# The last output chunk of a Sinkhorn-attention + bilinear-FFN kernel, written as one 128x512 piece instead of a 384-column and a 128-column piece

## The chip, the core and the metric

The kernel runs on one core of a Trainium2 chip. The metric is the device time in microseconds (us) of one execution; for the kernel before it is the median of three runs. A profiled execution gives the trace that all rows below come from.

## What is computed

The kernel computes block-sorted attention and feeds its output to a bilinear feed-forward layer. Batch 4, 8 heads, 768 positions, head size 64; the feed-forward layer sees 3072 tokens of width 512 and a hidden width of 1536.

```
P = sort_net                          # (4, 8, 8, 8), one 8x8 matrix a head
for _ in range(5):                    # Sinkhorn
    P = exp(P - max(P, -1)); P /= sum(P, -1) + 1e-9; P /= sum(P, -2) + 1e-9
k_sorted, v_sorted = P mixed over the 8 blocks of 96 positions of k and of v
attn = softmax(q_block @ k_sorted_block.T / 8)       # each block of 96 on its own
x    = (attn @ v_sorted_block), heads side by side    # (3072, 512)
out  = ((x @ w_a) * (x @ w_b)) @ w_out                # (3072, 512) float32
```

## The kernel before

All matmul operands are bfloat16; sums are float32 in PSUM. The batches 0 to 3 go one after the other through attention and feed-forward, and the attention of the next batch is woven between the feed-forward steps of the present one by a fixed order written out in the kernel (`paced`). The order of every engine is that of the code: the whole program stands in a manual schedule. GpSimd issues the loads, SyncE (SP) the transposes by DMA and the stores.

Batch 3 has no attention left to weave in, so its feed-forward runs alone. It has 24 `ffn_ab` steps (12 chunks of the hidden width times 2 halves of 384 tokens: eight 128x384 matmuls into two PSUM tiles `pf` at L343, a copy by ScalarE at L363, a product by VectorE into `hT` at L364) and then six `ffn_out` steps, one for each chunk `c` = 0 to 5 of 128 tokens. These six are the end of the kernel, and only they bear on what follows.

For chunks 0 to 4 of batch 3, `ffn_out` makes 12 accumulating matmuls (KO = 12) of 512 columns into one PSUM tile `po` (L386), copies the 128x512 float32 result to the SBUF tile `o_sb` (through the helper `copy`: L161 when ScalarE does it, for even `c`; L163 when VectorE does it, for odd `c`), and SyncE issues one DMA of 256 KB to the output (L399). `po` comes from the pool `psF` with four buffers, `o_sb` has three.

For the last chunk (batch 3, `c` = 5), `ffn_out` calls `ffn_last` instead (L380, L381). It handles the 512 output columns as two pieces, one after the other: columns 0 to 383 with 12 matmuls of 384 columns (L373), a ScalarE copy and a DMA on SyncE's queue (L377); then columns 384 to 511 with 12 matmuls of 128 columns, a VectorE copy and a DMA on ScalarE's queue (L377). It is the only DMA of the program that ScalarE issues.

After the last instruction of the program's own, the closing code follows (the profile gives it line L630): SyncE waits for the DMA semaphores one after the other, and then the engines meet, clear semaphores and meet again.

Of the kernel before, what the change touches and what calls it, by code (L numbers as in the profile page):

```python
# [9 lines left out]
FP32 = mybir.dt.float32  # L10
# [6 lines left out]
def _ap(t: bass.AP, extra_offset, pattern):  # L17
    return bass.AP(tensor=t.tensor, offset=t.offset + extra_offset,
                   ap=[list(p) for p in pattern])
# [3 lines left out]
def kernel(  # L23
# [11 lines left out]
    nc = tc.nc  # L35
    P = 128
    B, H, S, D = q.shape
# [3 lines left out]
    DMODEL = H * D  # L41
# [4 lines left out]
    NCH = S // P  # L46
    HP = H // 2
    KA = DMODEL // P
    KO = DFF // P
# [16 lines left out]
    ffp = ctx.enter_context(tc.tile_pool(name="ffp", bufs=2))  # L66
    psA = ctx.enter_context(tc.tile_pool(name="psA", bufs=2, space=PSUM))
    psF = ctx.enter_context(tc.tile_pool(name="psF", bufs=4, space=PSUM))
# [31 lines left out]
    w_out_sb = const.tile([P, KO, DMODEL], BF16, name="w_out_sb")  # L100
# [58 lines left out]
    def copy(eng, out, in_):  # L159
        if eng == "act":  # L160
            nc.scalar.copy(out=out, in_=in_)  # L161
        else:
            nc.vector.tensor_copy(out=out, in_=in_)  # L163
# [170 lines left out]
    hTs = {}  # L334
# [29 lines left out]
        nc.vector.tensor_mul(out=hT[:, m, t * HW:(t + 1) * HW], in0=a_sb,  # L364
                             in1=ab[1][:, 0:HW])

    def ffn_last(b, c):
        hT = hTs[b]
        rows = out[b * S:(b + 1) * S, :].rearrange("(p c) n -> c p n", c=NCH)
        for n0, n1, eng, queue in ((0, 384, "act", nc.sync), (384, DMODEL, "dve", nc.scalar)):  # L370
            po = psF.tile([P, 512], FP32, tag="F", name="po")
            for m in range(KO):
                nc.tensor.matmul(po[:, 0:n1 - n0], lhsT=hT[:, m, c * P:(c + 1) * P],  # L373
                                 rhs=w_out_sb[:, m, n0:n1], start=(m == 0), stop=(m == KO - 1))
            o_sb = ffp.tile([P, 512], FP32, tag="o_sb", name="o_sb", bufs=3)
            copy(eng, o_sb[:, 0:n1 - n0], po[:, 0:n1 - n0])
            queue.dma_start(out=rows[c][:, n0:n1], in_=o_sb[:, 0:n1 - n0])  # L377

    def ffn_out(b, c):
        if b == B - 1 and c == NCH - 1:  # L380
            ffn_last(b, c)  # L381
            return
        hT = hTs[b]
        po = psF.tile([P, DMODEL], FP32, tag="F", name="po")
        for m in range(KO):
            nc.tensor.matmul(po, lhsT=hT[:, m, c * P:(c + 1) * P], rhs=w_out_sb[:, m, :],  # L386
                             start=(m == 0), stop=(m == KO - 1))
        o_sb = ffp.tile([P, DMODEL], FP32, tag="o_sb", name="o_sb", bufs=3)
        copy("act" if c % 2 == 0 else "dve", o_sb, po)
        if b == 0:  # L390
            h, u = divmod(c, 3)
            for c2 in range(2):
                nc.sync.dma_start(
                    out=_ap(out, (h * PH * NCH + 2 * u + c2) * DMODEL,
                            [[NCH * DMODEL, PH], [1, DMODEL]]),
                    in_=o_sb[c2 * PH:(c2 + 1) * PH])
        else:
            rows = out[b * S:(b + 1) * S, :].rearrange("(p c) n -> c p n", c=NCH)
            nc.sync.dma_start(out=rows[c], in_=o_sb)  # L399


    with tc.manual_schedule(engines={ET.PE, ET.Pool, ET.SP}):
        with tc.manual_schedule(engines={ET.Activation, ET.DVE}):
# [7 lines left out]
            for it in range(5):  # L411
# [7 lines left out]
                if it == 2:  # L419
                    with nc.allow_low_precision("sum of one one and zeros"):  # L420
                        nc.vector.reduce_sum(
                            out=mask, in_=_ap(ident, 0, [[P, P], [1, CG], [CG, NB]]),
# [3 lines left out]
                if it > 0:  # L426
                    nc.tensor.matmul(heat[0:NB, 1, 0:NB], lhsT=rsum, rhs=rsum,
                                     start=True, stop=True)
# [8 lines left out]
                else:  # L437
                    nc.vector.tensor_mul(
                        out=p_fin.bitcast(BF16).rearrange("h (i j u) -> h i j u", i=NB, j=NB),
# [160 lines left out]
        for b in range(B):  # L600
            ab = [lambda m=m, t=t, b=b: ffn_ab(b, m, t)
                  for m in range(KO) for t in range(2) if b > 0 or t == 1]
            po = [lambda c=c, b=b: ffn_out(b, c) for c in range(NCH)]
            paced(ab, po, units_full(b + 1) if b + 1 < B else [], 3 if b == 0 else 2)
# [30 lines left out]
```

## Time and profile before

| what | value |
| --- | --- |
| median of 3 runs | 250.99 us (250.99 to 251.01) |
| the profiled execution's own time | 250.99 us |
| its span, first to last instruction | 249.2 us |
| what lies around the span | 1.8 us |
| granted TensorE clock | 1.000 of full |
| PE busy / VectorE busy / ScalarE busy | 239.0 us (96%) / 112.8 us (45%) / 102.8 us (41%) |
| stores by SyncE, 256 KB each (L399) | 17, landing 2.0 us after the issue (median) |

The profiled execution took as long as the median of the runs, so a sum made against its trace can be read as a change of the median. In rows of the profile, the engine comes first, then the line, the operation and the tiles (`out<-in`); a trailing q (SPq, ACTq) means the engine's sequencer, which issues DMAs and waits for semaphores. "Landing" is the time from the start of a DMA's issue to the update of its semaphore.

### The profile page before, as it was taken

The page shows a single profiled execution, that of the slowest core. Times are in us where ns is not written, and L with a number is a line of the kernel's source. Part 1 is how long each engine was busy: PE and PEld are TensorE (multiplying, and loading weights), DVE is VectorE, ACT ScalarE, POOL GpSimd, SP SyncE. Part 2 cuts the span into 40 slices and gives each one's busy share as a digit, 9 for nine tenths or more (in the row PEclk, how much of TensorE's full clock was granted, in tenths as well). Part 3 has the DMA queues.
Part 4 walks back from the last instruction along what each step waited for, and adds up shares of the span by engine and source line. Part 5 has one row for each costly group of instructions (what it writes and reads, how often), then busy time and mean ns, then how long its engine had stood idle before and what let it go on. Part 6 is the DMA issues. An engine that isn't in the chain of part 4 may idle for free.

```text
span 249.2 us, 5660 instructions
## 1 busy us (share of the span) xinstructions
PE 239.0 (96%) x2330; PEld 139.8 (56%) x2342; DVE 112.8 (45%) x267; ACT 102.8 (41%) x203; POOL 59.4 (24%) x83
## 2 busy tenths in 40 slices
PE   7789899999999999999999999999999999999994
PEld 2366566666655455666655456666645456655443
DVE  6774546655654323464633334363616144444110
ACT  3365656366633035636343146645440033333001
POOL 8975579439300002305061000000000000000000
PEclk9999999999999999999999999999999999999999
DMA  6999999999832869646584831232134310000122
GB/s 81 198 199 197 197 202 198 207 202 202 98 63 54 168 141 158 95 78 90 85 130 128 201 102 31 45 63 45 33 82 116 121 42 3 0 0 4 42 114 97
DMA packets 49162, 26.85 MB, mean 108 GB/s; under 512 B 25968, under 2 KB 46192, under 8 KB 49136
## 3 DMA queue, kind: packets, MB, share of 16 engines
q0 software_dynamic: 20944, 14.16, 39.0%
q1 hardware_dynamic: 28048, 12.27, 21.3%
q8 instruction: 18, 0.29, 0.5%
q10 hardware_dynamic: 144, 0.07, 0.1%
q14 instruction: 8, 0.07, 0.1%
HBM read 28.32 MB, written 6.29 MB: 139 GB/s over the span
## 4 chain that ended last, share of the span: by engine, by line
PE 90%; DMA 2%; POOL 2%; DVE 2%; issue 1%; ACT 1%; POOLq 0%; DVEq 0%
PE pf L343 50%; PE po L386 24%; PE mix L292 4%; PE o_ps L242 3%; DMA v<-in_v_dram 2%; PE sc L313 2%; PE mixh L192 1%; PE po L373 1%; PE vs_ps L282 1%; PE sc L207 1%; PE vs_ps L219 1%; PE q_ps L271 1%; PE xt_ps L233 1%; DVE hT L364 1%; DVE xph L248 1%
## 5 line engine op out<-in xcount | busy, mean ns | idle before, releaser
L364 DVE TENSOR_TENSOR hT<-a_sb,pf 128x384 bf16<-128x384 bf16 x95 | 52.5, 553 | 73.1 <-PE pf L343 49.2
L343 PE MATMUL pf<-xT,w_a_sb 128*128 128x384 bf16 x380 | 77.9, 327 | 0.0
L343 PE MATMUL pf<-xT,w_b_sb 128*128 128x384 bf16 x380 | 77.4, 326 | 0.0
L363 ACT CAST a_sb<-pf 128x384 bf16<-128x384 f32 x95 | 45.5, 479 | 63.9 <-PE pf L343 42.6
L386 PE MATMUL po<-w_out_sb,hT 128*128 128x512 bf16 x265 | 60.5, 379 | 0.6
L343 PEld LDWEIGHTS <-w_b_sb 128*128 128x128 bf16 x384 | 37.5, 98 | 24.9 <-issue 0.3
L343 PEld LDWEIGHTS <-w_a_sb 128*128 128x128 bf16 x384 | 34.9, 98 | 22.1
L386 PEld LDWEIGHTS <-hT 128*128 128x128 bf16 x276 | 26.4, 98 | 30.2
L161 ACT COPY o_sb<-po 128x512 f32<-128x512 f32 (+1 forms) x13 | 7.5, 577 | 50.5 <-PE po L386 49.1
L163 DVE COPY o_sb<-po 128x512 f32<-128x512 f32 (+1 forms) x12 | 7.9, 658 | 42.5 <-PE po L386 37.0
L318 ACT ACTIVATE eT<-sc 96x768 bf16<-96x768 f32 x24 | 18.1, 803 | 3.2 <-PE sc L313 3.2
L248 DVE TENSOR_TENSOR xp<-o_ps,rec 96x512 bf16<-96x512 f32 x24 | 15.7, 683 | 0.2
L161 ACT CAST kT<-mix 128x384 bf16<-128x384 f32 x24 | 10.3, 482 | 7.9 <-PE mix L292 7.9
L94 POOL DMA_DIRECT2D k<-in_k_dram x16 | 11.6, 728 | 6.1 <-PE pf L343 3.6
L94 POOL DMA_DIRECT2D v<-in_v_dram x16 | 11.6, 726 | 4.8 <-PE pf L343 3.1
L242 PEld LDWEIGHTS <-eT 96*128 96x128 bf16 x256 | 10.3, 97 | 3.3 <-ACT eT L211 0.7
L550 POOL COPY gate<-kT 1x1 bf16<-1x1 bf16 x4 | 0.7, 178 | 47.3 <-ACT kT L161 47.3
L242 PE MATMUL o_ps<-vs,eT 96*128 96x65 bf16 x256 | 11.2, 193 | 0.6 <-ACT eT L211 0.6
L94 POOL DMA_DIRECT2D q<-in_q_dram x12 | 8.7, 724 | 3.2 <-DMA w_out_sb<-in_moe_w_out_dram 1.6
L257 POOL COPY qc<-q 128x768 bf16<-128x768 bf16 x8 | 6.6, 842 | 8.1 <-DMA q<-in_q_dram 8.1
L167 PE MATMUL heat<-warm 128*128 128x512 bf16 x20 | 6.9, 484 | 1.4 <-DVE warm L77 1.3
L211 ACT ACTIVATE eT<-sc 96x768 bf16<-96x768 f32 x8 | 6.5, 808 | 3.3 <-PE sc L207 3.3
(81 smaller groups left out, 162.3 us busy)
## 6 DMA issues: line engine op xcount, KB each, us to landing
out_dram<-o_sb SPq DMA_DIRECT2D x17, 256.0 KB, 2.0
k<-in_k_dram POOLq DMA_DIRECT2D x16, 192.0 KB, 6.5
v<-in_v_dram POOLq DMA_DIRECT2D x16, 192.0 KB, 6.4
q<-in_q_dram POOLq DMA_DIRECT2D x12, 192.0 KB, 7.0
w_a_sb<-in_moe_w_a_dram POOLq DMA_DIRECT2D x6, 256.0 KB, 10.6
w_b_sb<-in_moe_w_b_dram POOLq DMA_DIRECT2D x6, 256.0 KB, 10.7
w_out_sb<-in_moe_w_out_dram POOLq DMA_DIRECT2D x3, 512.0 KB, 10.0
out_dram<-o_sb SPq DMA_DIRECT2D x12, 128.0 KB, 2.4
```

Source lines behind the costliest of these rows:

```text
L94: nc.gpsimd.dma_start(out=to, in_=_ap(t, base, [[W, P], [S * D, 2], [1, W]]))
L161: nc.scalar.copy(out=out, in_=in_)
L163: nc.vector.tensor_copy(out=out, in_=in_)
L167: nc.tensor.matmul(ps[:, 0:cols], lhsT=warm[:, 0:P], rhs=warm[:, 0:cols], start=True, stop=True)
L242: nc.tensor.matmul(o_ps[:, e, i * (D + 1):(i + 1) * (D + 1)], lhsT=eT[:, hf, e, i * BLK:i * BLK + P], rhs=vs[0:BLK, i0 + i, V0 - 1 + e * ( ...
L248: nc.vector.tensor_tensor(out=_ap(xp, i0 * 2 * D, [[nxp * 2 * D, BLK], [D, 2], [2 * D, NBH], [1, D]]), in0=_ap(o_ps, 1, [[1024, BLK], [511 ...
L292: nc.tensor.matmul(mix[e * D:(e + 1) * D, c // 3, c % 3 * P:(c % 3 + 1) * P], lhsT=src2[:, e, c * D:(c + 1) * D], rhs=s_all[:, 2 * g + e], ...
L318: nc.scalar.activation(out=eT[:, hf, :, 0:HB], in_=sc[0:BLK, :, 0:HB], func=AF.Exp, scale=float(scale))
L343: nc.tensor.matmul(pf[:, 0:HW], lhsT=w_sb[:, kc, m * P:(m + 1) * P], rhs=x_cols(b, kc, t), start=(kc == 0), stop=(kc == KA - 1))
L363: nc.scalar.copy(out=a_sb, in_=pf[:, 0:HW])
L364: nc.vector.tensor_mul(out=hT[:, m, t * HW:(t + 1) * HW], in0=a_sb, in1=ab[1][:, 0:HW])
L386: nc.tensor.matmul(po, lhsT=hT[:, m, c * P:(c + 1) * P], rhs=w_out_sb[:, m, :], start=(m == 0), stop=(m == KO - 1))
```

## The change

The function `ffn_last` and its call are taken out. The last chunk then goes through `ffn_out` as chunk 3 of the same batch does: 12 matmuls of 512 columns into one `po`, one VectorE copy of 128x512 (`c` = 5 is odd), and one DMA of 256 KB on SyncE's queue. Nothing else of the program is changed; before this chunk every engine has the same instructions in the same order. ScalarE loses one copy and its one DMA; SyncE issues as many DMAs as before.

```diff
-    def ffn_last(b, c):
-        hT = hTs[b]
-        rows = out[b * S:(b + 1) * S, :].rearrange("(p c) n -> c p n", c=NCH)
-        for n0, n1, eng, queue in ((0, 384, "act", nc.sync), (384, DMODEL, "dve", nc.scalar)):
-            po = psF.tile([P, 512], FP32, tag="F", name="po")
-            for m in range(KO):
-                nc.tensor.matmul(po[:, 0:n1 - n0], lhsT=hT[:, m, c * P:(c + 1) * P],
-                                 rhs=w_out_sb[:, m, n0:n1], start=(m == 0), stop=(m == KO - 1))
-            o_sb = ffp.tile([P, 512], FP32, tag="o_sb", name="o_sb", bufs=3)
-            copy(eng, o_sb[:, 0:n1 - n0], po[:, 0:n1 - n0])
-            queue.dma_start(out=rows[c][:, n0:n1], in_=o_sb[:, 0:n1 - n0])
-
     def ffn_out(b, c):
-        if b == B - 1 and c == NCH - 1:
-            ffn_last(b, c)
-            return
         hT = hTs[b]
         po = psF.tile([P, DMODEL], FP32, tag="F", name="po")
         for m in range(KO):
```

## The prediction

> **What bounds the kernel now.** I read the page's summary first, then the page's chain of work that ended last, then the same chain cut to the last 21 us, then the timeline of the last 8 us, and at last the waits of SyncE and the DMA issues of the closing stretch. The page says that the kernel as a whole is bound by TensorE:
>
> ```profile
> PE 239.0 (96%) x2330; PEld 139.8 (56%) x2342; DVE 112.8 (45%) x267; ACT 102.8 (41%) x203; POOL 59.4 (24%) x83
> PE 90%; DMA 2%; POOL 2%; DVE 2%; issue 1%; ACT 1%; POOLq 0%; DVEq 0%
> L163 DVE COPY o_sb<-po 128x512 f32<-128x512 f32 (+1 forms) x12 | 7.9, 658 | 42.5 <-PE po L386 37.0
> ```
>
> That share says nothing of the edit, which touches only the last chunk. The last row's mean of 658 ns mixes eleven copies of 128x512 with one of 128x128, so I do not use it. The chain, cut to its last 21 us, ends in pieces (start, duration, what) that are TensorE's last matmuls and then VectorE's copy alone:
>
> ```profile
> 243.43 2.63 PE po L373 x24
> 246.06 0.02 issue
> 246.08 0.29 DVE o_sb L163
> ```
>
> The timeline shows what lies beside them:
>
> ```profile
> 240.93 0.69 DVE L163 COPY o_sb<-po 128x512 f32<-128x512 f32 x1 [4.54 <-PE po L386]
> ...
> 243.26 2.78 PE L373 MATMUL po<-w_out_sb,hT 128*128 128x384 bf16 x24
> 243.46 0.59 ACT L161 COPY o_sb<-po 128x512 f32<-128x512 f32 x1 [4.59 <-PE po L386]
> 245.46 0.48 ACT L161 COPY o_sb<-po 128x384 f32<-128x384 f32 x1 [1.41 <-PE po L373]
> 245.96 0.33 SPq L377 DMA_DIRECT2D out_dram<-o_sb  x1
> 246.08 0.29 DVE L163 COPY o_sb<-po 128x128 f32<-128x128 f32 x1 [4.46 <-PE po L373]
> 246.41 0.38 ACTq L377 DMA_DIRECT2D out_dram<-o_sb  x1
> ```
>
> Its rows are start, duration, engine, what, and in brackets the idle time before and who ended it. TensorE runs without a gap into its last matmul; both copies wait for TensorE and not for a buffer. The first piece's copy and store begin 0.6 us before the second piece's copy: they lie beside TensorE's last 12 matmuls. Behind TensorE stand, in order, a copy of 128x128 (0.29 us), an issue, a landing, and the closing code. The waits of SyncE and the issues of the last 24 us say which landing the closing code waits for and how long a store takes:
>
> ```profile
> SPq L630 <- DMA out_dram<-o_sb: 1.5, 2, 1.3
> ```
>
> ```profile
> out_dram<-o_sb SPq DMA_DIRECT2D x5, 256.0 KB, 2.0
> out_dram<-o_sb SPq DMA_DIRECT2D x1, 192.0 KB, 1.9
> out_dram<-o_sb ACTq DMA_DIRECT2D x1, 64.0 KB, 1.6
> ```
>
> SyncE waits twice for output stores at the end (1.5 us in total). By the trace's records the 192 KB store lands at 247.83 us and the 64 KB store at 248.05 us, so the last landing is the small store's, and the span ends at 249.21 us: 1.15 us of closing code behind it. The landings in nanoseconds from issue are 2003 to 2042 for the five 256 KB stores and 1647 for the 64 KB one. So the end is one serial path: TensorE, second copy, its store, closing code. Each term of it is on the path in full.
>
> **The change part by part.** I follow that path and take differences.
>
> *Matmuls.* Before, 24 matmuls: the 384-column ones start 0.1625 us apart and the 128-column ones 0.056 us apart, together 12 x 0.2185 = 2.62 us of starts. After, 12 of 512 columns, which start 0.216 us apart in chunks 0 to 4: 2.59 us. The copy starts behind the last matmul's start by 0.256 us with 128 columns, and by 0.415 us (three copies) or 0.471 us (one, on VectorE) with 512. From the chunk's first matmul at 243.26 us to the copy that is now 246.08 - 243.26 = 2.82 us and then becomes 11 x 0.216 + 0.415 = 2.79 us, or 2.85 us. I take 0.00, with ends -0.03 and +0.03. Half the weight loads fall away (24 become 12); they cost nothing now, because the 24 lie beside matmuls that already run without a gap.
>
> *The last copy.* VectorE's copy grows from 128x128 to 128x512. The trace has both forms: 0.291 us and 0.692 us. Nothing covers it, since TensorE has ended: +0.40 us. The removed ScalarE copy (0.48 us) ended at 245.94 us, before TensorE's end, so taking it out gains nothing.
>
> *Waits for buffers.* The new copy takes the `o_sb` buffer that chunk 2 used, whose store was issued at 238.89 us and landed 2.0 us later, some 5 us before it is wanted. It also follows chunk 4's ScalarE copy, over at 244.05 us. Cost 0, hidden by 2 us or more of TensorE's work.
>
> *The last issue.* SyncE issues in place of ScalarE. Issues on SyncE started 0.024 to 0.028 us behind the end of their copies, ScalarE's 0.032 us: about 0.00. In front of it on SyncE's queue stands only chunk 4's store, issued at 244.07 us, and nothing but the closing code is queued behind it. ScalarE's issue of 0.38 us goes, and nobody waited for it other than through the landing.
>
> *The landing.* One store of 256 KB instead of 64 KB behind the copy. The nearest rows are the five stores of the same size, shape and queue from the same stretch: 2.01 us (median) against 1.65 us. +0.36 us, with ends +0.32 (if the 192 KB store's traffic beside it had held up the small one a little less than I think) and +0.41. The removed 192 KB store ended first and gains nothing. A price well above that would need other traffic; the slowest 256 KB store of the program took 4.6 us, among loads and transposes, and none of those is left at the end.
>
> The page "DMA: Bandwidth & Descriptors" of the Trainium skill, section "Rules for kernel authors", speaks for the change: it says to coalesce many small transfers into one large one. Its section "Anatomy of one DMA" gives about 2.0 us fixed for each DMA of GpSimd's path; if the two stores paid that in series, the change would save 2.0 us there and the sum would be near 249.4 us. The rows speak against that reading: the two landings, 1.87 and 1.65 us long, overlap and together last 2.09 us (245.96 to 248.05), so no fixed cost is paid twice on the path. By that section's other term, bytes over 436 GB/s, the landing would differ by 0.45 us instead of 0.36 and the sum would be 251.87 us (an estimate from that page).
>
> *Closing code.* SyncE checks its eight store semaphores one after the other, about 0.06 us each, in a fixed order. Now the last landing is that of the fourth check, with four to go; after the change SyncE's last store carries the semaphore of the third, with five to go. +0.06 us; ends 0 and +0.06. The rest (1.14 us from the fourth check to the end) stays.
>
> *Sum.* 0.00 + 0.40 + 0.00 + 0.36 + 0.06 = +0.82 us; with the matmul term at its more frequent row (-0.03) it is +0.79 us, which I take. The profiled execution took 250.99 us, the same as the median, so 250.99 + 0.79 = 251.78 us. Adding the low ends gives 250.99 - 0.03 + 0.40 + 0.32 + 0 = 251.68; the high ends give 250.99 + 0.03 + 0.40 + 0.41 + 0.06 = 251.89. About 0.2% (0.5 us) is what a measurement of this kernel can tell from no change, so the sum lies above that bound, not far.
>
> **The rivals.**
>
> *No change that can be told: the larger store costs nothing.* If a landing on quiet queues were all fixed latency, and 1.65 us for the small store only reflected a head start of its queue, just the copy would count: 250.99 + 0.40 = 251.39 us, within 0.2%. For it: 192 KB landed in 1.87 us and 64 KB in 1.65, so most of a landing does not depend on size. Against it: five rows of 256 KB, all at 2.0 us, are longer than both. 8 in 100.
>
> *Faster: ScalarE's DMA queue has a price outside the span.* The change removes the only DMA that ScalarE issues, and with it the queue (144 packets, q10 on the page). If the program pays for a second hardware queue in the 1.8 us around the span, all of that is the most it can save: 250.99 + 0.79 - 1.8 = 250.0 us. It decides from 0.79 + 0.5 = 1.3 us of saving on, that is, if over 70% of the time around the span were that queue's. For it: no row shows what fills that time. Against it: nothing in the span waits for that queue, and its one issue took 0.38 us, 0.05 more than SyncE's. 4 in 100.
>
> *Slower by more: the last store lands late.* If the last 256 KB store took what the slowest did, 4.6 us, the time would be 250.99 + 0.79 + 2.6 = 254.4 us; half of that excess gives 253.1. Against it: the last 21 us hold no other traffic of size. 4 in 100.
>
> *The change does not reach the end.* If another engine finished last, nothing would change. The chain and SyncE's wait for the store exclude it; 1 in 100, counted with the first rival.
>
> **How the numbers follow.** The forecast has 83 in 100: 251.78 us. The range begins at 251.4, where the first rival lies, and goes to 252.0, a tenth above the high ends, for small shifts around the span that no row bounds; it leaves out 1 to 2 in 10. Slower by over 0.2% (above 251.49): the forecast and the late store, 0.87. Within 0.2%: 0.09. Faster: 0.04.
>
> **What would show it right or wrong.** Right: the last VectorE copy has the form 128x512 with 0.69 us and starts within 0.05 us of 246.08; SyncE issues 256 KB about 0.03 us behind its end, near 246.8; it lands 2.0 us later; five checks follow, and the span is 250.0 us. Wrong: a landing under 1.8 us, or a time around the span that is no longer 1.8 us, or a start of the last copy that moved by over 0.1 us, which would mean that something before the last chunk shifted.

## The result, and the profile after

| | before | after |
| --- | --- | --- |
| median of 6 runs each, on one chip | 251.00 us (250.99 to 251.25) | 251.84 us (251.58 to 252.10) |
| profiled execution: time / span | 250.99 / 249.21 us | 251.84 / 250.05 us |
| time around the span | 1.78 us | 1.79 us |

The ratio is 1.0032, with a 95% interval of 1.0019 to 1.0045: the kernel became 0.84 us slower, about 0.3%. The interval leaves out "no change"; its low end, 0.19%, lies just under the 0.2% that one measurement can tell. Run times of one kernel fall into steps some 0.25 us apart, and two of the traces below run 0.27 to 0.28 us later than the kernel before from the 19th microsecond of the span on, long before anything that was changed. So single terms are read from the last chunk's rows and not from run times.

The last pieces of the chain that ended last (start, duration, what), of the kernel after:

```profile
241.53 4.49 PE po L371 x20
246.02 0.04 DVEq L163
246.06 0.04 issue
246.10 0.69 DVE o_sb L163
```

It has the same shape as before: TensorE, then VectorE's copy alone. The last piece is 0.69 us instead of 0.29 us long, and it begins at 246.10 instead of 246.08 us. A new piece of 0.04 us stands ahead of it, VectorE's own sequencer (DVEq). Beside it, rows of the timeline:

```profile
243.46 0.59 ACT L161 COPY o_sb<-po 128x512 f32<-128x512 f32 x1 [4.59 <-PE po L371]
246.10 0.69 DVE L163 COPY o_sb<-po 128x512 f32<-128x512 f32 x1 [4.49 <-PE po L371]
246.82 0.33 SPq L384 DMA_DIRECT2D out_dram<-o_sb  x1
```

No store is issued between 244.4 and 246.82 us, where before 192 KB were on their way from 245.96 us on. The waits of SyncE at the end, and the DMA issues after 245.5 us (queue, count, KB, us to landing):

```profile
SPq L615 <- DMA out_dram<-o_sb: 1.5, 1, 1.5
```

```profile
out_dram<-o_sb SPq DMA_DIRECT2D x1, 256.0 KB, 2.0
```

SyncE now waits once, for the one store, 1.5 us long. It landed 2.017 us behind its issue; the closing code behind it took 1.215 us where it had taken 1.154.

All terms of the path, in us, as the two traces' records have them, from chunk 4's ScalarE copy (243.46 us in both) to the end of the span:

| | before | after | difference | predicted |
| --- | --- | --- | --- | --- |
| from chunk 4's copy to the start of the last copy | 2.620 | 2.645 | +0.025 | -0.03 (+0.03 by the other row) |
| last copy | 0.291 | 0.692 | +0.401 | +0.40 |
| its end to the issue of the last store | 0.032 | 0.027 | -0.005 | 0.00 |
| landing of the last store | 1.647 | 2.017 | +0.370 | +0.36 |
| closing code | 1.154 | 1.215 | +0.061 | +0.06 |
| sum | 5.744 | 6.596 | +0.852 | +0.79 |

The span itself grew by 0.846 us, since chunk 4's copy began 0.006 us earlier. Each trace is one execution, but the rows come back in the traces of the experiments below: a last store of 256 KB lands 2.016 to 2.023 us behind its issue in all five versions that have one, a last one of 64 KB, issued 0.44 to 0.45 us behind another, 1.632 to 1.650 us in three. The closing code takes 1.210 to 1.220 us where five checks follow the last landing, and 1.154 and 1.169 us where four do.

### The profile page after: what moved, and what is told of

Read it like the earlier page. It is cut to its first block, busy times and chain, and to the rows that moved or that the text cites. A ratio compares the mean times of both kernels' runs of the same rounds, so it can differ in the third digit from the quotient of the medians.

```text
span 250.1 us, 5634 instructions
## 1 busy us (share of the span) xinstructions
PE 239.0 (96%) x2318; PEld 139.1 (56%) x2330; DVE 113.2 (45%) x267; ACT 102.3 (41%) x202; POOL 59.4 (24%) x83
## 3 DMA queue, kind: packets, MB, share of 16 engines
HBM read 28.32 MB, written 6.29 MB: 138 GB/s over the span
## 4 chain that ended last, share of the span: by engine, by line
PE 90%; DMA 3%; DVE 2%; POOL 2%; issue 1%; ACT 1%; POOLq 0%; DVEq 0%
PE pf L343 50%; PE po L371 25%; PE mix L292 4%; PE o_ps L242 3%; DMA v<-in_v_dram 3%; PE sc L313 2%; PE mixh L192 1%; PE vs_ps L282 1%; PE sc L207 1%; PE vs_ps L219 1%; PE q_ps L271 1%; PE xt_ps L233 1%; DVE hT L364 1%; DVE xph L248 1%; POOL k L94 1%
## 5 line engine op out<-in xcount | busy, mean ns | idle before, releaser
L371 PE MATMUL po<-w_out_sb,hT 128*128 128x512 bf16 x277 | 63.1, 379 | 0.6
L371 PEld LDWEIGHTS <-hT 128*128 128x128 bf16 x288 | 27.5, 98 | 31.6
L163 DVE COPY o_sb<-po 128x512 f32<-128x512 f32 x12 | 8.3, 691 | 42.6 <-PE po L371 41.4
L161 ACT COPY o_sb<-po 128x512 f32<-128x512 f32 x12 | 7.0, 586 | 49.1 <-PE po L371 49.1
```

## The experiments

The theory: the end is one serial path, and copy, landing and closing checks each count in full. The rivals: a landing does not depend on size; ScalarE's DMA queue has a price around the span; the closing checks or the copy lie beside something else. "Path" below is the stretch of the table's sum, from chunk 4's ScalarE copy to the end of the span: 5.74 us before, 6.60 us after.

**The last copy on ScalarE.** The kernel after, one engine changed.

```diff
-        copy("act" if c % 2 == 0 else "dve", o_sb, po)
+        last = b == B - 1 and c == NCH - 1
+        copy("act" if c % 2 == 0 or last else "dve", o_sb, po)
```

> The kernel after, with the last 128x512 copy on ScalarE instead of VectorE (its other rows of this shape: 0.586 against 0.692 us). Theory (the end is one serial path, the copy counts in full): 0.11 us less for the copy, and 0.00 to 0.06 us less because ScalarE's copies of 512 columns started 0.415 us behind the last matmul's start and VectorE's 0.471; 251.84 - 0.11 to 0.17 = 251.67 to 251.73 us. Rival (the landing or the closing code absorbs the copy): 251.84 us.

The timeline:

```profile
246.10 0.58 ACT L161 COPY o_sb<-po 128x512 f32<-128x512 f32 x1 [2.05 <-PE po L371]
246.71 0.33 SPq L385 DMA_DIRECT2D out_dram<-o_sb  x1
```

The copy is 0.107 us shorter and the path 6.47 us, 0.126 us under the kernel after. The profiled execution took 251.70 us, as expected. The median did not: it was 251.84 us, the rival's value, between two groups of three runs at 251.7 and 252.0 us, beside 251.12 us of the kernel before measured with it (+0.72 us). So the run times leave this open, and the rows decide: the copy counts in full. The other part of the expectation fell: ScalarE's copy starts nearly as late as VectorE's had, 0.461 us behind the last matmul's start and 2.634 us behind chunk 4's copy. The later start does not belong to VectorE.

**One store, two copies.** The kernel before, with both copies into one tile and one store on SyncE behind the second.

```diff
+        o_sb = ffp.tile([P, 512], FP32, tag="o_sb", name="o_sb", bufs=3)
         for n0, n1, eng, queue in ((0, 384, "act", nc.sync), (384, DMODEL, "dve", nc.scalar)):
...
-            o_sb = ffp.tile([P, 512], FP32, tag="o_sb", name="o_sb", bufs=3)
-            copy(eng, o_sb[:, 0:n1 - n0], po[:, 0:n1 - n0])
-            queue.dma_start(out=rows[c][:, n0:n1], in_=o_sb[:, 0:n1 - n0])
+            copy(eng, o_sb[:, n0:n1], po[:, 0:n1 - n0])
+        nc.sync.dma_start(out=rows[c], in_=o_sb)
```

> The kernel before, with its two matmul pieces and its two copies kept, but both copies into one tile and one 256 KB store on SyncE behind the second copy: the store's part of the change alone. Theory (landing and closing check count, copy stays at 0.29 us): second copy ends at 246.37 us, issue 246.40, landing 2.02 us later at 248.42, 1.215 us of closing code, span 249.63, time 251.42 us, that is +0.43 on the kernel before. Rival (a landing on quiet queues does not depend on size): +0.06, 251.05 us.

Timeline and issues:

```profile
246.42 0.29 DVE L163 COPY o_sb<-po 128x128 f32<-128x128 f32 x1 [4.52 <-PE po L374]
246.77 0.33 SPq L377 DMA_DIRECT2D out_dram<-o_sb  x1
```

```profile
out_dram<-o_sb SPq DMA_DIRECT2D x1, 256.0 KB, 2.0
```

The path is 6.27 us, 0.52 us over the kernel before: landing 2.017 us (+0.37) and closing code 1.219 us (+0.065) as expected, and 0.09 us that was not. The second copy starts 0.056 us later, and the store is issued 0.062 us behind it instead of 0.032. Both now wait for ScalarE as well, through the shared tile; a separate semaphore instruction ahead of each takes over the wait for the engine that did end last. By run times it was 251.51 us beside 251.12 us, +0.39 us, a ratio of 1.0019 (1.0010 to 1.0027). The rival of a landing without regard to size, +0.06 us, is out.

**One copy, two stores at once.** The kernel after, with its last store cut in two.

```diff
-            nc.sync.dma_start(out=rows[c], in_=o_sb)
+            if b == B - 1 and c == NCH - 1:
+                nc.sync.dma_start(out=rows[c][:, 0:384], in_=o_sb[:, 0:384])
+                nc.scalar.dma_start(out=rows[c][:, 384:DMODEL], in_=o_sb[:, 384:DMODEL])
+            else:
+                nc.sync.dma_start(out=rows[c], in_=o_sb)
```

> The kernel after, with its one copy of 128x512 kept, but its result stored by two DMAs issued at about the same time: columns 0 to 383 on SyncE, 384 to 511 on ScalarE. Theory (what counts is the bytes that are left to move behind the copy, whatever the queues): the later of the two lands 2.0 to 2.1 us behind the issue, the closing code has one check less behind it, 251.75 to 251.87 us. Rival (each store pays for its own size alone): landings of 1.87 and 1.65 us, 251.84 - 0.15 = 251.69 us or less. Rival (a second hardware queue has a price outside the span): the time around the span grows above 1.78 us.

Timeline and issues:

```profile
246.82 0.33 SPq L385 DMA_DIRECT2D out_dram<-o_sb  x1
246.83 0.37 ACTq L386 DMA_DIRECT2D out_dram<-o_sb  x1
```

```profile
out_dram<-o_sb SPq DMA_DIRECT2D x1, 192.0 KB, 2.1
out_dram<-o_sb ACTq DMA_DIRECT2D x1, 64.0 KB, 2.3
```

This is slower than one store: the path is 6.84 us, 0.25 us over the kernel after, and the median 252.07 us beside 251.12. The 64 KB store landed 2.258 us behind its issue, where the same store took 1.647 us when it was issued 0.45 us after SyncE's. Both the theory's 2.0 to 2.1 us and the rival's 1.65 us were wrong here. The landing's bytes alone do not set it: two stores that are issued together delay each other. Of the 0.61 us more, the packet records put 0.18 us ahead of the store's first packet, 0.26 us into the time in which its packets move, together with those of the 192 KB, and 0.17 us behind its last packet. The time around the span was 1.78 us as before. The expected saving of a check was wrong as well, since ScalarE's store got the semaphore checked third; the closing code took 1.214 us.

**Both stores on SyncE.** The kernel before, without any DMA by ScalarE.

```diff
-        for n0, n1, eng, queue in ((0, 384, "act", nc.sync), (384, DMODEL, "dve", nc.scalar)):
+        for n0, n1, eng, queue in ((0, 384, "act", nc.sync), (384, DMODEL, "dve", nc.sync)):
```

> The kernel before, with its second piece's store on SyncE's queue too, so that ScalarE issues no DMA in the whole program. Theory (the queue as such costs nothing): SyncE's issue of the first store (245.96 to 246.29 us) is over before the second copy ends at 246.37, so 250.95 to 251.05 us as before, and 1.78 us around the span. Rival (ScalarE's queue has a price outside the span, up to 1.8 us): under 250.95 by that price, with less than 1.78 us around the span. Rival (two stores on one queue go one after the other): 0.1 to 0.4 us over 250.99.

Its issues:

```profile
out_dram<-o_sb SPq DMA_DIRECT2D x1, 192.0 KB, 1.9
out_dram<-o_sb SPq DMA_DIRECT2D x1, 64.0 KB, 1.6
```

The profiled execution took 250.98 us with 1.77 us around the span, and the path is 5.76 us against 5.74. The median, 251.24 us beside 251.12, lies above the expected range and inside that of the rival of two stores in series, but the ratio is 1.0005 (0.9997 to 1.0014), and the rows show no such series: the 64 KB store landed 1.650 us behind its issue on SyncE's queue, 1.647 us on ScalarE's. So a landing's length goes with the store's size and not with its queue, and ScalarE's queue has no price that these rows show. In its section "Issuing engines are not separate DMA queues" the page "DMA: Bandwidth & Descriptors" of the Trainium skill says that issuing from several engines saves only sequencer time, and these rows agree.

**ScalarE's queue used ahead of the last store.** The kernel after, with chunk 4's store on ScalarE's queue.

```diff
-            nc.sync.dma_start(out=rows[c], in_=o_sb)
+            queue = nc.scalar if b == B - 1 and c == NCH - 2 else nc.sync
+            queue.dma_start(out=rows[c], in_=o_sb)
```

> The kernel after, with chunk 4's store (not the last one) issued by ScalarE instead of SyncE, so that ScalarE's DMA queue is used and the last chunk's path is as in the kernel after. Theory (the queue as such costs nothing in or around the span): as the kernel after, 0.8 us over the kernel before, 1.78 us around the span. Rival (the queue has a price around the span): more than 1.78 us around the span.

251.84 us beside 251.02, a ratio of 1.0041 (1.0023 to 1.0059); the profiled execution took 251.82 us, with 1.77 us around the span and a path of 6.60 us. With both directions tried, the rival of the queue is out.

**More stores, so that the last one carries the semaphore checked last.** The kernel after, with n = 5, and the kernel before, with n = 4:

```diff
-            nc.sync.dma_start(out=rows[c], in_=o_sb)
+            if b == B - 1 and c < n:
+                for c2 in range(2):
+                    nc.sync.dma_start(out=rows[c][c2 * PH:(c2 + 1) * PH],
+                                      in_=o_sb[c2 * PH:(c2 + 1) * PH])
+            else:
+                nc.sync.dma_start(out=rows[c], in_=o_sb)
```

> The kernel after, with the stores of chunks 0 to 4 of batch 3 each cut into two of 64 partitions: five more stores by SyncE, so that the last store carries the semaphore that the closing code checks last instead of third. Theory (each check behind the last landing costs 0.06 us on the path): no check follows the landing's own, 5 x 0.061 = 0.31 us less in the closing code, landing to end of span 0.91 us instead of 1.215; the five added issues (0.33 us each) lie beside 2.6 us of matmuls a chunk. About 251.84 - 0.31 = 251.53 us where the kernel before has 251.0. Rival (the checks run beside something else that ends the span): landing to end stays 1.2 us and the time 251.84.

> The kernel before, with the stores of chunks 0 to 3 of batch 3 each cut into two of 64 partitions: four more stores, so that ScalarE's last store carries the semaphore checked last instead of fourth. Theory: 4 x 0.061 = 0.24 us less behind the landing (0.91 instead of 1.154 us), 0.24 us under the kernel before in the same call, some 250.75 to 250.9 us; faster than both kernels. Rival (checks not on the path): as the kernel before.

SyncE's closing instructions from 248.5 us on (count, duration in ns, first and last start), of the kernel after and then of the one with five more stores:

```profile
L615 SPq EVENT_SEMAPHORE  x8: 17/28/28, 248.9 to 250.0; - x8
```

```profile
L620 SPq EVENT_SEMAPHORE  x3: 17/17/28, 248.9 to 249.7; - x3
```

The first count is six checks and the two meetings of the engines; the second is one check and the two meetings. Five checks have moved ahead of the landing, and the last start comes 0.3 us sooner while the first is the same. The closing code took 0.906 us instead of 1.215, and the median was 251.54 us beside 251.02. The halved stores took 0.47 to 0.60 us to issue, not 0.33; they lie beside matmuls all the same, and the last copy starts no later.

The other version's timeline and issues:

```profile
246.23 0.34 SPq L377 DMA_DIRECT2D out_dram<-o_sb  x1
246.68 0.37 ACTq L377 DMA_DIRECT2D out_dram<-o_sb  x1
```

```profile
out_dram<-o_sb ACTq DMA_DIRECT2D x1, 64.0 KB, 1.6
```

Its closing code took 0.927 us instead of 1.154, and its path 5.50 us instead of 5.74. By run times it was 250.97 us beside 251.02, with a ratio of 0.9989 (0.9981 to 0.9998), so the expected 250.75 to 250.9 us was not met. By median it is the fastest version here, but its gain of about 0.1% is below what one measurement of this kernel can tell; the path's rows carry it (-0.24 us). In its trace everything from the 19th microsecond on ran 0.27 us later, which hides the gain in the profiled execution's time.

**The cut at column 416, with four more stores.**

```diff
-        for n0, n1, eng, queue in ((0, 384, "act", nc.sync), (384, DMODEL, "dve", nc.scalar)):
+        for n0, n1, eng, queue in ((0, 416, "act", nc.sync), (416, DMODEL, "dve", nc.scalar)):
```

> As the kernel before with four more stores, and the last chunk cut at column 416 instead of 384. Theory, if 96-column matmuls start as fast as their columns stream (0.042 us): the second copy is 0.03 us shorter (1.04 ns a column from the rows of 512 and 128 columns), its store of 48 KB lands some 0.03 us sooner, in all 0.06 us less than with the cut at 384. If a matmul cannot start sooner than 0.056 us behind the one before, as the 128-column ones did: 12 x 0.014 = 0.16 us more on TensorE's end, so 0.10 us more than with the cut at 384.

Timeline and issues:

```profile
246.08 0.26 DVE L163 COPY o_sb<-po 128x96 f32<-128x96 f32 x1 [4.46 <-PE po L373]
246.14 0.34 SPq L377 DMA_DIRECT2D out_dram<-o_sb  x1
246.37 0.37 ACTq L377 DMA_DIRECT2D out_dram<-o_sb  x1
```

```profile
out_dram<-o_sb SPq DMA_DIRECT2D x1, 208.0 KB, 1.9
out_dram<-o_sb ACTq DMA_DIRECT2D x1, 48.0 KB, 1.9
```

The matmuls of 96 columns did start 0.042 us apart, and the copy was 0.033 us shorter. But the 48 KB store landed 1.859 us behind its issue, 0.23 us later than the 64 KB store in the version with the cut at 384. The first store was now issued 0.228 us ahead of it and not 0.447. By the packet records the delay stands ahead of the first packet (1.157 us behind the issue instead of 0.914); the packets then moved in 0.317 us instead of 0.378, so their shorter rows, 384 bytes instead of 512, are not the main cause. The path is 5.68 us against 5.50, and the median 251.17 us beside 251.02, ratio 1.0000 (0.9991 to 1.0008). What was gained in the copy was lost, and more, to two stores that were issued too close.

## Why the prediction was right

The forecast of 251.78 us was 0.06 us off. That the medians agree so closely is in part luck: the ratio's interval reaches from 0.5 to 1.1 us. What carries the account is the path, +0.85 us by the rows where +0.79 was forecast. Its steps, one by one:

- *The last copy* was priced by the row of the same form at +0.40 us and measured +0.401. That it has no cover was shown by moving it to ScalarE: 0.107 us less on the copy, 0.126 us less on the path.
- *The landing* was priced at +0.36 us and measured +0.370. One store in place of two, with nothing else changed in size, gave the same +0.370.
- *The closing checks* were priced at +0.06 us and measured +0.061. Turning the order of the semaphores by five took 0.309 us off, by four 0.227 us.
- *The matmul term* is where the 0.06 us lie. The prediction had two rows for the start of a copy behind a chunk's last 512-column matmul, 0.415 us (four copies by the records, not three) and 0.471 us. It wrote down 0.00 with ends of -0.03 and +0.03, took -0.03, the more frequent row, into its sum, and left the other to the range. It was the other: +0.025 us. The prediction took the two rows for a spread; in the traces the difference goes with the way a copy's waits are carried (below). The one late row was chunk 3's, the chunk that the last one now resembles.
- *The buffers* were free, as argued: TensorE ended the last copy's wait, not a store.

One reading was loose and changes no term: of the first piece only the copy begins 0.6 us ahead of the second piece's copy. Its store is issued 0.12 us ahead (245.96 against 246.08 us) and lies mostly behind TensorE's end; it takes no time of its own because it lands 0.22 us before the small one.

Of the rivals, the landing without regard to size fell with the single store. The queue's price outside the span fell with both runs on it: 1.77 to 1.79 us lie around the span with and without ScalarE's queue. A late landing did not come.

## What to carry to other kernels

At the end of a kernel, walk the last piece alone: last matmul, copy, issue, landing, closing checks. Here nothing covered any of these, and each could be priced from a row of the same size elsewhere in the trace. Cutting the last output into a large first piece and a small last one saved copy and landing behind TensorE's end. The two issues should stay apart. At 0.45 us the small store landed in 1.65 us; at 0.23 us it took 0.23 us longer, and the cut still paid: a path of 5.68 us against 6.29 us for one store whose semaphore is checked last as well (the kernel after with five more stores). With one copy and both stores issued behind it, cutting the store cost 0.25 us.

## What was not expected

Two stores issued close together delay each other. By the trace's packet records, the first packet of ScalarE's store came 0.91 us behind its issue when SyncE's had been issued 0.45 us ahead, 1.16 us with 0.23 us between, and 1.09 us with 0.005 us between. Landings were 1.65, 1.86 and 2.26 us for 64, 48 and 64 KB. At 0.23 us all of the delay stands ahead of the first packet; with both issued at once most of it stands behind, where the packets of both stores move together. What the two share was not tried apart.

A copy's start goes with the way its waits are carried. In the kernel before, VectorE's last copy waited with its own instruction for TensorE and started 0.256 us behind the last matmul's start. In the kernel after, the wait for TensorE sits in a separate semaphore instruction ahead of the copy, which is the row "0.04 DVEq" of the chain, and the copy itself waits for ScalarE, done long before. The start came 0.471 us behind the last matmul's instead of the 0.415 us of chunk 4's copy, and ScalarE's copy in the same place came nearly as late. The ten traces hold no exception in the last batch: every 512-column copy that waits for TensorE itself starts 0.415 to 0.418 us behind the last matmul's start, every one with a separate instruction for that wait 0.461 to 0.472 us, chunk 3's copy in the kernel before among them. The 128-column copy went from 0.256 to 0.313 us when the shared tile moved its wait for TensorE in the same way. So the late start could have been read from the trace of the kernel before. That the place of the wait is the cause, and not something else that these copies share, such as their wait for ScalarE, was not tried by itself.
